# Attention and two expert layers on one core: a written order for TensorE in the first attention units, no filler matmuls, half of their copies on VectorE, narrower score weights

## The chip, the cores and the metric

The kernel runs on one core of a Trainium2 chip. The metric is the device time of one execution in microseconds. Engines are named as in the profile: PE is TensorE (PEld its weight loads), DVE VectorE, ACT ScalarE, POOL GpSimd, SP SyncE, whose queue issues nearly all transfers.

## What is computed

Inputs are q, k, v of shape (4, 8, 576, 64) and p of shape (4, 8, 32, 64), all f32.

```python
def sm_attn(qq, kk, vv):
    s = scale * np.matmul(qq, kk.transpose(0, 1, 3, 2))
    a = np.exp(s - np.max(s, axis=-1, keepdims=True))
    a = a / (np.sum(a, axis=-1, keepdims=True) + 1e-09)
    return np.matmul(a, vv)
p_packed = sm_attn(p, k, v)              # 32 packed rows per head
out = sm_attn(q, p_packed, p_packed)     # the 576 queries attend to them
x = out as (2304, 512)
h = x @ w_in                             # 512 x 2048
x = softplus(h) @ w_out                  # 2048 x 512
out = (sigmoid(x @ w_gate) * (x @ w_val)) @ w_out2    # 512 x 1536, 1536 x 512
```

## The kernel before

**Attention.** There are eight units u, one for each batch b and group g of four heads. `attn_unit(u)` is a generator of eleven stages: k is copied chunk by chunk on POOL (`by_chunk`, the tile x), transposed on PE and copied from PSUM to kT (`tr_pair`, two head pairs, one stage each, all copies on ACT as E1 is ACT); the scores of p against k (L403) go to the PSUM tile s1, of which DVE takes the maximum; ACT makes the exponential a1, DVE normalises it; q is transposed in the same way; a1 is transposed to a1T (L437); pp = a1T times v (L456) is the packed p, which ACT copies into the block diagonal tile bdT, and POOL from there into ppq (L472), whose layout holds all four batches side by side; scores of q against bdT (s2, L486), whose softmax a2 runs over DVE, ACT and POOL; last, a2 is transposed (L514) and kept as a high part A2h and a low part A2l. In the units u < WARM (3), `warm` adds six 128x128 matmuls on the identity behind pp (L381): their result goes nowhere.

**The first expert layer.** h and the product with w_out go in chunks c of 256 columns; an entry (b, c) makes two `emit_h` groups (twelve matmuls L113 to L115 each, three for each product of high and low parts) and, two groups later, the `emit_out1` of the group (L725, L726, L728, 24 matmuls), whose sums DVE adds to xa (L733). p_packed is folded into the weights: the wp of an entry are w_in times the packed rows. For c = 0 and 1 `prep_wp_one` does that for each batch (L591), for c = 3 and up `prep_wp_four(c)` does it for all four: eight matmuls of ppq with w_in (L645) in two groups, an ACT copy of each bank into a cv tile (L652), sixteen small transfers from cv to xs that put each batch's rows in place (L656), and then, in `split_wp`, POOL's high part wph (L104) and low part wpl (L101).

**Order.** Two weight buffers `raw` hold the raw words of w_in and w_out; `load_next` puts the next load on SP's queue at the end of each conversion (three DVE steps, L180, L185, L189, over a PSUM bank from some point on), since the load reuses the buffer that the conversion has emptied. Converted w_out is rounded by ACT (woh, L108) and its low part made on POOL (wol, L101). All of this is cut into generators, called jobs: `tick()` runs one step of the first job in the queue, and `between` does one tick behind every quarter of an output product. `finish("wp03")` and its like run all ticks that are still missing as soon as an entry needs its weights. Attention units get their stages from `att_tick`, which picks the next unit that is ready. The framework then orders the instructions of each engine's queue by priorities of its own, except where `tc.keep_in_program_order` pins an instruction; so an engine's order is read from the compiled program, not from the source alone.

The start is `while not att_done(1): att_tick(L0)`, with a tick each from the seventeenth on. PSUM has eight banks: four single ones (`bank1`, PSUM tile ps) that rotate, and two double ones (`bank2`).

Of the kernel before, what the change touches and what calls it, by code (L numbers as in the profile page):

```python
# [9 lines left out]
F32 = mybir.dt.float32  # L10
# [3 lines left out]
AF = mybir.ActivationFunctionType  # L14
ALU = mybir.AluOpType
# [6 lines left out]
def attn_moe_moe_kernel(  # L22
# [68 lines left out]
    def bank1():  # L91
        return ps_o[-1].tile([P, 512], F32, tag="o", name="ps1")
# [245 lines left out]
    RELD = 0  # L338
    SUMP = 0
    E1 = nc.scalar  # L340
    WARM = 3
    FOUR = 3
    SPC = 2

    def heads(tile_, start, step):
# [11 lines left out]
        )  # L357
        return x

    def tr_pair(src, j, dst, eng):  # L360
        x = by_chunk(src, j)
        for hf in range(2):
            ps = bank1()
            for c in range(3):
                nc.tensor.transpose(
                    ps[:, c * CT : (c + 1) * CT],
                    x[:, 3 * hf + c].rearrange("p h d -> p (h d)"),
                    ident[:CT, :CT],
                )
# [13 lines left out]
    def attn_unit(u):  # L383
        b, g = divmod(u, 2)
        half, odd = divmod(b, 2)
        px = bank1()
        nc.tensor.transpose(px[:, :P], praw.pop(u).rearrange("p i d -> p (i d)"), ident)
# [7 lines left out]
        tr_pair(kt, 0, kT, nc.scalar)  # L395
# [14 lines left out]
        mx = att.tile([P, 4], F32, tag="mx", bufs=2, name="mx")  # L410
        nc.vector.tensor_reduce(mx[:, 0:1], s1[:, :, :HS], op=ALU.max, axis=AX.XY)
        nc.vector.tensor_scalar(mx[:, 1:2], mx[:, 0:1], -SC, None, op0=ALU.mult)
# [9 lines left out]
        else:  # L422
            nc.vector.tensor_scalar(a1, a1, mx[:, 3:4], None, op0=ALU.mult)
        yield
        qt = kqv.pop(("q", u))
        qT = att.tile([P, 2, S], F32, tag="qT", bufs=2, name="qT")
        tr_pair(qt, 0, qT, nc.scalar)
        yield
        tr_pair(qt, 1, qT, E1)
        done_kqv("q", u)  # L430
        yield
        a1T = att.tile([CT, NC, P], F32, tag="a1T", bufs=2, name="a1T")
        for hf in range(2):
            pa = bank1()
            for c in range(3):
                o = (3 * hf + c) * CT
                nc.tensor.transpose(pa[:CT, c * P : (c + 1) * P], a1[:, o : o + CT], ident)  # L437
            nc.scalar.activation(
                a1T[:, 3 * hf : 3 * hf + 3].rearrange("p c n -> p (c n)"),
                pa[:CT, : 3 * P], AF.Copy,  # L440
            )
        yield
        vt = kqv.pop(("v", u))
        pp = bank1()
        for j in range(2):
            for c in range(NC):
                if u >= VCH:
                    nc.tensor.matmul(
                        pp[:, 64 * j : 64 * j + 64],
                        vt[:, c, 2 * j : 2 * j + 2].rearrange("p h d -> p (h d)"),  # L450
                        a1T[:, c, 64 * j : 64 * j + 64], start=c == 0, stop=c == NC - 1,
                    )
                    continue
                for e in range(2):
                    n0 = 64 * j + 32 * e
                    nc.tensor.matmul(  # L456
                        pp[64 * e : 64 * e + 64, 64 * j + 32 * e : 64 * j + 32 * e + 32],
                        vt[:, 2 * j + e, c, :],
                        a1T[:, c, n0 : n0 + 32],
                        start=c == 0,  # L460
                        stop=c == NC - 1,
                    )
        done_kqv("v", u)
        warm(u, pp[:, 3 * P :], 6)
        for e in range(2):
            r = slice(64 * e, 64 * e + 64)
            to = bdT[r].rearrange("p j n -> p (j n)")
            copy(
                BDA, heads(to, 512 * half + 256 * g + 64 * odd + 32 * e, 64 if odd else 192),
                heads(pp[r], 32 * e, 64),  # L470
            )
            nc.gpsimd.tensor_scalar(  # L472
                ppq[r, 2 * g : 2 * g + 2, b],
                heads(to, 512 * half + 256 * g + 64 * odd + 32 * e, 64 if odd else 192),
                1.0, 0.0, op0=ALU.mult, op1=ALU.add,
            )
        yield
        a2s = []
        for hf in range(2):
            s2 = bank1()  # L480
            for c in range(3):
                for j in range(2):
                    slot = odd ^ j
                    o = c * P + 64 * slot
                    t = (3 * hf + c) * CT
                    nc.tensor.matmul(  # L486
                        s2[:CT, o : o + 64],
                        qT[:, j, t : t + CT],
                        bdT[:, 4 * half + 2 * g + j, 64 * slot : 64 * slot + 64],
                        start=True,  # L490
                        stop=True,
                    )
# [18 lines left out]
        for hf in range(2):  # L511
            pt = bank1()
            for c in range(3):
                nc.tensor.transpose(  # L514
                    pt[:, c * CT : (c + 1) * CT], a2s[hf][:, c * P : (c + 1) * P],
                    ident[:CT, :CT],
                )
# [16 lines left out]
    def att_done(u):  # L534
        return att_left(u) == 0
# [2 lines left out]

    def ready(u, n):
        return n not in NEEDS or (NEEDS[n], u) in kqv  # L540

    def att_tick(last=2 * B):

# [88 lines left out]

    xs = {}

    def prep_wp_four(c):

        wt = w_in_f[c]
# [272 lines left out]
    units.extend(range(2 * B))  # L910
    n = 0
    jobs.append(("win0", prep_win(0)))
    while not att_done(1):
# [244 lines left out]
```

## Time and profile before

| | |
|---|---|
| time of 3 runs | 861.76 us median (861.45 to 863.3) |
| the profiled execution | 862.72 us, its span 860.6 us |
| PE busy | 839.2 us (98%) |
| DVE busy | 588.4 us (68%) |
| POOL busy | 479.8 us (56%) |
| ACT busy | 326.5 us (38%) |
| moved by transfers | 90.79 MB, 105 GB/s in the mean |

The span runs from the first to the last instruction. A busy share is a mean over stages that differ: in the first 42 us PE waits for loads and for the other engines, from then on it works nearly without a pause until the end.

### The profile page before, as it was taken

The numbers are of one execution on the slowest core, as the hardware profiler recorded it, in microseconds if no ns is written. First come the engines' busy times: TensorE is split into PE (matmuls) and PEld (weight loads), VectorE is DVE, ScalarE is ACT, GpSimd is POOL, SyncE is SP. The second block draws the span as 40 slices with busy tenths as digits, with TensorE's granted clock in tenths as the row PEclk, the third lists the DMA queues.
The fourth block names the chain that finished last, engine by engine and source line by source line (L and its number), as shares of the span: only waits on it lengthen the run. The fifth ranks groups of instructions, "written<-read, shape, count | busy, mean of one in ns | idle before, by whom it ended". The sixth has DMA issues, their size and how long they took to land. (4 is left out here: it accounts for less than half of the span.)

```text
span 860.6 us, 15689 instructions
## 1 busy us (share of the span) xinstructions
PE 839.2 (98%) x6112; PEld 783.0 (91%) x6112; DVE 588.4 (68%) x1004; ACT 326.5 (38%) x606; POOL 479.8 (56%) x469
## 2 busy tenths in 40 slices
PE   7899999999999999999989999999999999999997
PEld 5788989899989999999989999999989999999996
DVE  2776556946656375458788688897896656767665
ACT  4467575563333333434323422232352432322210
POOL 4564333245647364594579786886983734536400
PEclk9999999999999999999999999999999999999999
DMA  9984320203363233500155464644525412213003
GB/s 236 222 206 103 84 59 26 74 25 108 114 178 101 73 98 82 167 5 1 37 171 156 151 177 149 191 129 136 159 55 154 122 41 84 68 43 111 13 1 110
DMA packets 61864, 90.79 MB, mean 105 GB/s; under 512 B 7648, under 2 KB 40544, under 8 KB 61792
## 3 DMA queue, kind: packets, MB, share of 16 engines
q1 hardware_dynamic: 60784, 88.56, 36.9%
q10 hardware_dynamic: 1008, 1.25, 0.4%
q8 instruction: 48, 0.79, 0.4%
q14 instruction: 24, 0.20, 0.1%
HBM read 65.67 MB, written 18.87 MB: 98 GB/s over the span
## 5 line engine op out<-in xcount | busy, mean ns | idle before, releaser
L113 PE MATMUL bank<-aop,BH 128*128 128x288 f32 x672 | 199.1, 296 | 5.0 <-DVE work L1026 2.1
L115 PE MATMUL bank<-aop,BL 128*128 128x288 f32 x672 | 198.6, 296 | 0.0
L114 PE MATMUL bank<-aop,BH 128*128 128x288 f32 x672 | 197.8, 294 | 0.2 <-DVE aop L101 0.2
L733 DVE TENSOR_TENSOR xa<-xa,ps 128x288 f32<-128x288 f32 x224 | 99.5, 450 | 100.3 <-PE ps L728 100.1
L101 POOL TENSOR_TENSOR ghl<-g,ghl 128x576 fp32r<-128x576 f32 x64 | 93.5, 1463 | 132.1 <-ACT ghl L108 113.1
L725 PE MATMUL ps<-ghl,woh 128*128 128x288 f32 x512 | 146.4, 301 | 2.0 <-ACT cv L652 1.3
L726 PE MATMUL ps<-ghl,wol 128*128 128x288 f32 x512 | 143.6, 295 | 0.0
L113 PEld LDWEIGHTS bank<-aop,BH 128*128 128x128 f32 x672 | 126.2, 188 | 10.8 <-issue 2.5
L114 PEld LDWEIGHTS bank<-aop,BH 128*128 128x128 f32 x672 | 126.4, 188 | 4.2 <-DVE aop L101 0.4
L115 PEld LDWEIGHTS bank<-aop,BL 128*128 128x128 f32 x672 | 126.6, 188 | 0.0
L101 POOL TENSOR_TENSOR BL<-cv,BH 128x512 fp32r<-128x512 f32 (+1 forms) x96 | 117.2, 1235 | 3.4 <-ACT BH L108 2.4
L728 PE MATMUL ps<-ghl,woh 128*128 128x288 f32 x512 | 109.1, 294 | 0.1
L725 PEld LDWEIGHTS ps<-ghl,woh 128*128 128x128 f32 x512 | 96.2, 188 | 5.6 <-ACT cv L652 1.6
L726 PEld LDWEIGHTS ps<-ghl,wol 128*128 128x128 f32 x512 | 96.3, 188 | 0.2
L1026 DVE TENSOR_TENSOR work<-work,bank 128x576 f32<-128x576 f32 (+1 forms) x100 | 70.8, 725 | 31.5 <-PE bank L115 31.3
L1074 PE MATMUL ps<-ol,gv 128*128 128x512 f32 x216 | 84.9, 393 | 0.0
L1073 PE MATMUL ps<-oh,gv 128*128 128x512 f32 x216 | 84.3, 390 | 0.5 <-ACT gv L1039 0.4
L1075 PE MATMUL ps<-oh,gv 128*128 128x512 f32 x216 | 84.7, 393 | 0.0
L728 PEld LDWEIGHTS ps<-ghl,woh 128*128 128x128 f32 x512 | 82.2, 188 | 0.5 <-POOL ghl L101 0.5
L1081 DVE TENSOR_TENSOR xa<-xa,ps 128x512 f32<-128x512 f32 x90 | 61.5, 683 | 28.5 <-PE ps L1075 28.0
L104 POOL TENSOR_SCALAR BH<-cv 128x512 fp32r<-128x512 f32 (+1 forms) x48 | 30.0, 634 | 88.1 <-PE bank L114 87.8
L113 PE MATMUL ps<-A2h,wph 128*128 128x288 f32 x256 | 77.3, 302 | 0.4 <-ACT wph L595 0.4
(137 smaller groups left out, 1613.7 us busy)
## 6 DMA issues: line engine op xcount, KB each, us to landing
cv<-B SPq DMA_DIRECT2D x52, 256.0 KB, 2.7
B<-cv SPq DMA_DIRECT2D x48, 256.0 KB, 4.1
raw_in<-in_moe_w_in_dram SPq DMA_DIRECT2D x16, 512.0 KB, 3.7
raw_out<-in_moe_w_out_dram SPq DMA_DIRECT2D x16, 512.0 KB, 3.5
raw_g<-in_moe_w_gate_dram SPq DMA_DIRECT2D x12, 512.0 KB, 4.1
raw_v<-in_moe_w_val_dram SPq DMA_DIRECT2D x12, 512.0 KB, 4.4
raw_o<-in_moe_w_out_dram SPq DMA_DIRECT2D x12, 512.0 KB, 4.1
xs<-cv SPq DMA_DIRECT2D x80, 64.0 KB, 2.0
```

Of the source, the lines that this page charges most:

```text
L101: eng.tensor_tensor(lo, x, hi.bitcast(F32), op=ALU.subtract)
L113: nc.tensor.matmul(ps, wh, xh, start=first, stop=False)
L114: nc.tensor.matmul(ps, wh, xl, start=False, stop=False)
L115: nc.tensor.matmul(ps, wl, xh, start=False, stop=last)
L725: nc.tensor.matmul(out_, wh[:, ms], gh[:, f], start=f == 0, stop=False)
L726: nc.tensor.matmul(out_, wl[:, ms], gh[:, f], start=False, stop=False)
L728: nc.tensor.matmul(out_, wo_hl[c, f][0][:, ms], gl[:, f], start=False, stop=f == 1)
L733: nc.vector.tensor_tensor(dst, dst, out_, op=ALU.add)
L1026: nc.vector.tensor_tensor(to, x, y, op=ALU.add)
L1073: nc.tensor.matmul(bank, gh[:, ts_], oh, start=f == 0, stop=False)
L1074: nc.tensor.matmul(bank, gh[:, ts_], ol, start=False, stop=False)
L1075: nc.tensor.matmul(bank, gl[:, ts_], oh, start=False, stop=f == 1)
```

## The change

The change has five parts. (1) `FIRST` is a string that names, digit by digit, the unit whose next stage comes next, for the first 25 stages; `att_step` runs them, and while they last the PE instructions of units 0 to 2 are pinned to program order. Unit 1 (`AFIRST`) transposes its a1 ahead of its q. (2) WARM goes to 0: no fillers (FILL is empty). (3) In units 0 and 1 (`BYDVE`) DVE copies the second head pair of k and of q and the second half of a1T, which ACT did. (4) The scores of p take 64 columns of weights at a time and put each head pair into its own 64 partitions of s1, where before 128 columns, of which half belong to zeros, were accumulated over both pairs. (5) The copies into ppq leave `attn_unit` and become `prep_ppq`, eight steps ahead of `prep_wp_four` in the job of c = 3. The branch on VCH goes; its condition u >= 8 never held.

```diff
-    WARM = 3
+    WARM = 0
     FOUR = 3
+    FILL = {}
+    BYDVE = 2
+    AFIRST = (1,)
+    FIRST = "0001110000111101" + "222" + "000111"
+    pin = {u: False for u in range(2 * B)}
...
+    def pe(on, ins):
+        if on:
+            tc.keep_in_program_order(ins)
...
+        second = nc.vector if u < BYDVE else E1
...
-        tr_pair(kt, 1, kT, E1)
+        tr_pair(u, kt, 1, kT, second)
...
         for hf in range(2):
             for j in range(2):
-                nc.tensor.matmul(
-                    s1[:, hf, :HS],
-                    pT[u % 2][:, P * j : P * j + P],
+                r = slice(64 * j, 64 * j + 64)
+                pe(pin[u], nc.tensor.matmul(
+                    s1[r, hf, :HS],
+                    pT[u % 2][:, 192 * j : 192 * j + 64],
                     kT[:, j, hf * HS : (hf + 1) * HS],
-                    start=j == 0,
-                    stop=j == 1,
-                )
+                    start=True,
+                    stop=True,
+                ))
...
+                copy(
+                    hf == 0 or u >= BYDVE,
+                    a1T[:, 3 * hf : 3 * hf + 3].rearrange("p c n -> p (c n)"),
+                    pa[:CT, : 3 * P],
+                )
+        if u in AFIRST:
+            weights()
+            yield
...
-            nc.gpsimd.tensor_scalar(
-                ppq[r, 2 * g : 2 * g + 2, b],
-                heads(to, 512 * half + 256 * g + 64 * odd + 32 * e, 64 if odd else 192),
-                1.0, 0.0, op0=ALU.mult, op1=ALU.add,
-            )
...
+    def prep_ppq():
+        for b in range(B):
+            half, odd = divmod(b, 2)
+            for e in range(2):
+                r = slice(64 * e, 64 * e + 64)
+                for g in range(2):
+                    src = heads(
+                        bdT[r].rearrange("p j n -> p (j n)"),
+                        512 * half + 256 * g + 64 * odd + 32 * e, 64 if odd else 192,
+                    )
+                    pool_hi(ppq[r, 2 * g : 2 * g + 2, b], src)
+                yield
...
         if half == 0:
+            if c == FOUR:
+                yield from prep_ppq()
             yield from prep_wp_four(c)
...
+    for n, x in enumerate(FIRST):
+        for u in pin:
+            pin[u] = n < len(FIRST) and u <= 2
+        att_step(int(x))
+        if n > NW:
+            tick()
...
     while not att_done(1):
         att_tick(L0)
-        n += 1
-        if n > NW:
-            tick()
+        tick()
```

The change moves instructions at two places of the program: in the first 45 us or so, and around the weights job of c = 3, a quarter of the way through. Elsewhere every engine's order is the same as before.

The first place is DVE's order in the start, up to wpl of the first entry (cv and woh there are w_out of c = 0, mx and a the softmax of unit 2's scores, A2l the low parts of units 0 and 1). Before:

```order
L411 TENSOR_REDUCE mx<-ps_500 128x1
L101 TENSOR_TENSOR A2l_117<-ps_513,A2h_113 128x288
L412 TENSOR_SCALAR mx<-mx 128x1
L185 SCALAR_TENSOR_TENSOR cv<-raw_out,cv 128x512
L101 TENSOR_TENSOR A2l_117<-ps_519,A2h_113 128x288
L418 TENSOR_SCALAR mx<-mx 128x1
L189 SCALAR_TENSOR_TENSOR cv<-raw_out,cv 128x512
L419 RECIPROCAL mx<-mx 128x1
L101 TENSOR_TENSOR wpl<-ps_527,wph 128x512
```

And in the changed kernel, from the first conversion of w_in's second half on, and up to wpl:

```order
L180 TENSOR_SCALAR w_in<-raw_in 128x4x128
L514 TENSOR_REDUCE m_374<-ps_367 96x12
...
L438 RECIPROCAL mx<-mx 128x1
L101 TENSOR_TENSOR A2l_117<-ps_497,A2h_113 128x288
L442 TENSOR_SCALAR a_471<-a_471,mx 128x576
L189 SCALAR_TENSOR_TENSOR w_in<-raw_in,w_in 128x4x128
L101 TENSOR_TENSOR A2l_117<-ps_503,A2h_113 128x288
L180 TENSOR_SCALAR cv<-raw_out 128x512
L185 SCALAR_TENSOR_TENSOR cv<-raw_out,cv 128x512
L189 SCALAR_TENSOR_TENSOR cv<-raw_out,cv 128x512
L101 TENSOR_TENSOR wpl<-ps_511,wph 128x512
```

The conversion of w_in's second half ends late, behind most of the softmax work of units 0 and 1, and all three steps of the first w_out conversion stand ahead of wpl; from the maximum (L514) to wpl there are 36 instructions.

The second place is SP's queue around the transfers of the weights job of c = 3 (raw_in and raw_out are the loads of c = 3 and 4, raw_g the first one of the second expert layer). Before:

```order
L155 DMA raw_out<-in_moe_w_out_dram 128x1024 x2
L157 DMA raw_in<-in_moe_w_in_dram 128x4x256 x2
L656 DMA xs<-cv 32x512 x16
L155 DMA raw_out<-in_moe_w_out_dram 128x1024 x2
L157 DMA raw_g<-in_moe_w_gate_dram 128x4x256
```

And in the changed kernel:

```order
L155 DMA raw_out<-in_moe_w_out_dram 128x1024 x2
L157 DMA raw_in<-in_moe_w_in_dram 128x4x256 x2
L699 DMA xs<-cv 32x512 x8
L155 DMA raw_out<-in_moe_w_out_dram 128x1024
L699 DMA xs<-cv 32x512
L155 DMA raw_out<-in_moe_w_out_dram 128x1024
L699 DMA xs<-cv 32x512 x7
L157 DMA raw_g<-in_moe_w_gate_dram 128x4x256
```

The two raw_out loads move from behind the sixteen xs transfers to between them.

The third is POOL's order at the same place: ghl is the low part of a softplus result, on which an output product waits. Before:

```order
L101 TENSOR_TENSOR ghl<-g_2848,ghl 128x576
L104 TENSOR_SCALAR wph<-xs 128x512
L101 TENSOR_TENSOR wpl<-xs,wph 128x512
L104 TENSOR_SCALAR wph<-xs 128x512
L101 TENSOR_TENSOR wpl<-xs,wph 128x512
L104 TENSOR_SCALAR wph<-xs 128x512 x2
L101 TENSOR_TENSOR wpl<-xs,wph 128x512 x2
L101 TENSOR_TENSOR ghl<-g_2912,ghl 128x576
```

And in the changed kernel:

```order
L101 TENSOR_TENSOR ghl<-g_2792,ghl 128x576
L101 TENSOR_TENSOR wol<-cv,woh 128x512
L104 TENSOR_SCALAR wph<-xs 128x512
L101 TENSOR_TENSOR wol<-cv,woh 128x512
L101 TENSOR_TENSOR wpl<-xs,wph 128x512
L104 TENSOR_SCALAR wph<-xs 128x512 x2
L101 TENSOR_TENSOR wpl<-xs,wph 128x512 x2
L104 TENSOR_SCALAR wph<-xs 128x512
L101 TENSOR_TENSOR wpl<-xs,wph 128x512
L101 TENSOR_TENSOR ghl<-g_2898,ghl 128x576
```

The two wol of the next chunk, which stood behind three of the following ghl, now stand ahead of the first wph and of the first wpl. On PE, at the same place, the two groups of four weights matmuls (L645 before, L688 after) had 22 other matmuls between them and now have none; from the second group to the first L113 that reads the new wph there were 66 matmuls, and now there are 48.

## Rows read from the trace of the kernel before

**Rows 1.** The profile's page: busy time of PE, and the granted clock in 40 slices.

```profile
PE 839.2 (98%) x6112; PEld 783.0 (91%) x6112; DVE 588.4 (68%) x1004; ACT 326.5 (38%) x606; POOL 479.8 (56%) x469
...
PEclk9999999999999999999999999999999999999999
```

**Rows 2.** Windows: length, busy us (instructions) by engine, PE clock, DMA share, GB/s.

```profile
0.00:20.00 20.00, 15.61 (x98) 10.54 (x98) 3.30 (x9) 8.95 (x26) 9.30 (x17) 1.00 0.97 232
20.00:42.00 22.00, 18.88 (x219) 15.76 (x219) 17.68 (x45) 10.57 (x32) 11.28 (x15) 1.00 1.00 223
...
100.00:160.00 60.00, 59.53 (x587) 55.10 (x587) 38.74 (x93) 35.11 (x78) 21.52 (x26) 1.00 0.21 51
...
210.00:225.00 15.00, 15.00 (x112) 14.13 (x112) 7.47 (x18) 5.26 (x9) 6.64 (x7) 1.00 0.45 124
```

**Rows 3.** Timeline, all engines, 39 to 43 us: start, duration, what, idle before.

```profile
40.16 0.67 DVE L101 TENSOR_TENSOR wpl<-ps,wph 128x512 fp32r<-128x512 f32 x1
...
42.25 0.38 PE L115 MATMUL ps<-A2h,wpl 128*128 128x288 f32 x1
```

**Rows 4.** Timeline of PE, 50 to 52.5 us.

```profile
50.50 1.60 PE L381 MATMUL ps<-ident 128*128 128x128 f32 x12
```

**Rows 5.** Waits, 0 to 45 us: in total, times, longest.

```profile
ACT bdT L96 <- PE ps L381: 4.7, 2, 2.4
```

**Rows 6.** Groups of PE instructions by form, 42 to 165 us: busy us, mean ns.

```profile
L403 PE MATMUL ps<-kT,pT 128*128 128x288 f32 x40 | 10.7, 410 | 0.0
L591 PE MATMUL ps<-w_in,bdT 128*64 128x256 f32 x56 | 6.9, 386 | 0.2 <-ACT qT L372 0.2
```

**Rows 7.** Timeline of SP's queue, 0 to 46 us.

```profile
24.87 0.38 SPq L237 DMA_DIRECT2D xa<-in_q_dram  x1
```

**Rows 8.** Timeline of DVE, 21 to 28 us.

```profile
22.07 0.42 DVE L180 TENSOR_SCALAR w_in<-raw_in 128x512 int32<-128x512 int32 x1
```

**Rows 9.** Timeline of PE, 210 to 226 us.

```profile
210.01 1.24 PE L645 MATMUL ps<-w_in,ppq 64*128 64x256 f32 x8
...
214.30 1.13 PE L645 MATMUL ps<-w_in,ppq 64*128 64x256 f32 x8
...
224.20 0.29 PE L113 MATMUL ps<-A2h,wph 128*128 128x288 f32 x1
```

**Rows 10.** Timeline of SP's queue, 200 to 235 us.

```profile
211.84 11.01 SPq L656 DMA_DIRECT2D xs<-cv  x16
225.65 4.94 SPq L155 DMA_DIRECT2D raw_out<-in_moe_w_out_dram  x2
```

**Rows 11.** Timeline of POOL, 220 to 232 us.

```profile
222.49 0.62 POOL L104 TENSOR_SCALAR wph<-xs 128x512 fp32r<-128x512 f32 x1 [1.49 <-DMA xs<-cv]
223.19 1.29 POOL L101 TENSOR_TENSOR wpl<-xs,wph 128x512 fp32r<-128x512 f32 x1
```

**Rows 12.** Groups by form, 205 to 250 us, of DVE.

```profile
L185 DVE SCALAR_TENSOR_TENSOR ps<-raw_out,ps 128x512 int32<-128x512 int32 x4 | 2.8, 696 | 0.1
```

**Rows 13.** Groups by form, 205 to 250 us, of ACT.

```profile
L108 ACT ACTIVATE woh<-cv 128x512 fp32r<-128x512 f32 x4 | 2.5, 628 | 4.7 <-DVE cv L189 4.7
```

**Rows 14.** Groups by form, 205 to 250 us, of POOL.

```profile
L101 POOL TENSOR_TENSOR ghl<-g,ghl 128x576 fp32r<-128x576 f32 x8 | 11.4, 1431 | 13.1 <-ACT ghl L108 12.1 <-POOL wol L101 1.0
L101 POOL TENSOR_TENSOR wol<-cv,woh 128x512 fp32r<-128x512 f32 x4 | 5.2, 1294 | 1.7 <-ACT woh L108 1.7
```

**Rows 15.** The page's transfers: count, KB each, median us from issue to landing.

```profile
raw_out<-in_moe_w_out_dram SPq DMA_DIRECT2D x16, 512.0 KB, 3.5
...
xs<-cv SPq DMA_DIRECT2D x80, 64.0 KB, 2.0
```

**Rows 16.** Timeline of PE, 244 to 250 us.

```profile
248.02 0.40 PE L725 MATMUL ps<-ghl,woh 128*128 128x288 f32 x1 [1.32 <-ACT cv L652]
```

**Rows 17.** Waits, 205 to 250 us.

```profile
DVE ps L180 <- DMA raw_out<-in_moe_w_out_dram: 0.4, 2, 0.2
```

**Rows 18.** Waits of PE, 8 us to the end.

```profile
PE bank L113 <- DVE work L1026: 2.1, 2, 1.7
```

More of the change, by code (lines that the diff above doesn't have):

```diff
@@ L358, in by_chunk, with tr_pair @@
         return x
-    def tr_pair(src, j, dst, eng):
+    def pe(on, ins):
+        if on:
+            tc.keep_in_program_order(ins)
+    def tr_pair(u, src, j, dst, eng, fill=0):
+        on = pin[u]
         x = by_chunk(src, j)
@@ L363, in tr_pair @@
             ps = bank1()
+            for _ in range(0 if hf else fill):
+                pe(on, nc.tensor.matmul(
+                    ps[:, 320:], hot[:, :P], hot[:, 320:], start=True, stop=True
+                ))
             for c in range(3):
-                nc.tensor.transpose(
+                pe(on, nc.tensor.transpose(
                     ps[:, c * CT : (c + 1) * CT],
@@ L368, in tr_pair @@
                     ident[:CT, :CT],
-                )
+                ))
             o = dst[:, j, hf * HS : (hf + 1) * HS]
@@ L386, in attn_unit @@
         px = bank1()
-        nc.tensor.transpose(px[:, :P], praw.pop(u).rearrange("p i d -> p (i d)"), ident)
+        pe(pin[u], nc.tensor.transpose(
+            px[:, :P], praw.pop(u).rearrange("p i d -> p (i d)"), ident
+        ))
         for e in range(2):
@@ L392, in attn_unit @@
             )
+        second = nc.vector if u < BYDVE else E1
         kt = kqv.pop(("k", u))
         kT = att.tile([P, 2, S], F32, tag="kT", bufs=1, name="kT")
-        tr_pair(kt, 0, kT, nc.scalar)
+        tr_pair(u, kt, 0, kT, nc.scalar, FILL.get(("k", u), 0))
         yield
-        tr_pair(kt, 1, kT, E1)
+        tr_pair(u, kt, 1, kT, second)
         done_kqv("k", u)
@@ L424, in attn_unit, with weights @@
         yield
+        a1T = att.tile([CT, NC, P], F32, tag="a1T", bufs=2, name="a1T")
+        def weights():
+            for hf in range(2):
+                pa = bank1()
+                for c in range(3):
+                    o = (3 * hf + c) * CT
+                    pe(pin[u], nc.tensor.transpose(
+                        pa[:CT, c * P : (c + 1) * P], a1[:, o : o + CT], ident
+                    ))
+                copy(
[6 more added lines that the diff above has]
+            yield
         qt = kqv.pop(("q", u))
         qT = att.tile([P, 2, S], F32, tag="qT", bufs=2, name="qT")
-        tr_pair(qt, 0, qT, nc.scalar)
+        tr_pair(u, qt, 0, qT, nc.scalar, FILL.get(("q", u), 0))
         yield
-        tr_pair(qt, 1, qT, E1)
+        tr_pair(u, qt, 1, qT, second)
         done_kqv("q", u)
         yield
[L432 to L442, printed above, removed]
+        if u not in AFIRST:
+            weights()
+            yield
         vt = kqv.pop(("v", u))
@@ L446, in attn_unit @@
             for c in range(NC):
[L447 to L453, printed above, removed]
                 for e in range(2):
                     n0 = 64 * j + 32 * e
-                    nc.tensor.matmul(
+                    pe(pin[u], nc.tensor.matmul(
                         pp[64 * e : 64 * e + 64, 64 * j + 32 * e : 64 * j + 32 * e + 32],
@@ L461, in attn_unit @@
                         stop=c == NC - 1,
-                    )
+                    ))
         done_kqv("v", u)
@@ L470, in attn_unit @@
                 heads(pp[r], 32 * e, 64),
-            )
-            nc.gpsimd.tensor_scalar(
-                ppq[r, 2 * g : 2 * g + 2, b],
-                heads(to, 512 * half + 256 * g + 64 * odd + 32 * e, 64 if odd else 192),
-                1.0, 0.0, op0=ALU.mult, op1=ALU.add,
             )
@@ L485, in attn_unit @@
                     t = (3 * hf + c) * CT
-                    nc.tensor.matmul(
+                    pe(pin[u], nc.tensor.matmul(
                         s2[:CT, o : o + 64],
@@ L491, in attn_unit @@
                         stop=True,
-                    )
+                    ))
             s2v = s2[:CT, : 3 * P].rearrange("p (x n) -> p x n", n=NK)
@@ L513, in attn_unit @@
             for c in range(3):
-                nc.tensor.transpose(
+                pe(pin[u], nc.tensor.transpose(
                     pt[:, c * CT : (c + 1) * CT], a2s[hf][:, c * P : (c + 1) * P],
                     ident[:CT, :CT],
-                )
+                ))
             hi = A2h[b][:, g, hf * HS : (hf + 1) * HS]
@@ L540, in ready, with att_step @@
         return n not in NEEDS or (NEEDS[n], u) in kqv
+    def att_step(u):
+        if u in units:
+            units.remove(u)
+            live.append([attn_unit(u), 0, u])
+        x = next(y for y in live if y[2] == u)
+        next(x[0])
+        x[1] += 1
+        if x[1] == STAGES:
+            live.remove(x)
     def att_tick(last=2 * B):
@@ L633, in attn_moe_moe_kernel @@
     xs = {}
+    def prep_ppq():
[9 more added lines that the diff above has]
+                    pool_hi(ppq[r, 2 * g : 2 * g + 2, b], src)
+                yield
     def prep_wp_four(c):
@@ L912, in attn_moe_moe_kernel @@
     jobs.append(("win0", prep_win(0)))
+    for n, x in enumerate(FIRST):
[4 more added lines that the diff above has]
+            tick()
+    for u in pin:
+        pin[u] = False
     while not att_done(1):
         att_tick(L0)
-        n += 1
-        if n > NW:
-            tick()
+        tick()
     jobs.append(("wp00", prep_wp_one(0, 0)))
```

1 line of the change is left out of this document (added).

## The prediction

> **What bounds the kernel now.** I read the page first: PE is busy 839.2 us of 860.6 and its granted clock stands at 9 or more tenths in every slice [rows 1], so only PE time that goes or PE idle time that comes can move the end. Then the windows by stage [rows 2]: PE idles 4.4 us of the first 20 and 3.1 of the next 22, but 0.47 of the 60 from 100 to 160, and nothing at all from 210 to 225. So before about 42 us the start is a race of loads and VectorE work; behind it a microsecond of matmuls taken out of attention is a microsecond gained, and a stall put in is one lost. Next the timeline where the first h group gets going [rows 3]: L113 and L114 of h(0,0) have run, and its first L115 starts at 42.25, behind VectorE's wpl (40.16 + 0.67) and the transposes that stand between. From there PE hardly waits. The middle of the kernel I read last, since the order shows that the change reaches it.
>
> **What is removed.** Fillers: two groups of twelve passes stand in the start, and the third at 50.50 [rows 4], where PE is the bound; its row is 1.60 us long with the tail of its last pass, under which the next work begins, so I take 1.4. The first two cost ACT 4.7 us of waiting before its bdT copies [rows 5], which belongs to the start-up chain below and is not counted twice. The branch on VCH was never taken: nothing.
>
> **Scores.** Eight passes of L403 a unit: 40 passes are 10.7 us from 42 to 165, 2.14 a unit. The new shape (64 weight columns, alternating halves of the PSUM rows) has no row of its own; the nearest is L591, 64 weight columns into alternating halves, 56 passes in 6.9 us [rows 6], 0.123 each over 256 columns. For 288 columns that is 0.139, 1.1 us a unit. Bounds: nothing gained, if the halves don't overlap; 1.03 us a unit if they do wholly. L591 alternates its halves as the new rows will, so I take near the upper end, 0.85 (busy time counts the tail of a group's last pass, and switching remains). Five units lie where PE is the bound: 4.3 us (0 to 5.2). The three in the start hang on loads and count there.
>
> **Start-up order.** In the new order q of unit 2 is loaded ahead of raw_out, where before it stood behind it in SP's queue until 24.87 [rows 7]; the VectorE chain that ends in wpl is what the first L115 will wait for. That chain can't begin ahead of the second conversion of raw_in, which now started at 22.07 as soon as its load was there [rows 8]: the new order puts it ahead of the maximum of the first s2, and counting its 0.42 the 36 instructions from there to wpl start at about 22.5. VectorE did 45 instructions in 17.68 us busy of the 22 from 20 to 42 [rows 2], 0.39 each: 36 are 14.1 us, so wpl ends at 36.6 without any wait, and with the same share of waiting (22.0/17.68) at 40.0. Nothing tells which end is nearer; I take the middle, 38.3, and L115 moves there from 42.25: 4.0 us gained (2.2 to 5.6). VectorE's ten copies for units 0 and 1 (about 0.39 each by the same row, 3.9 us) fall into the first 22 us, of which it is busy 3.30 in the first 20 [rows 2]; if that cover were gone they would delay the chain by up to their 3.9 us, and this term would be nothing. The gains are 1.4 + 4.3 + 4.0 = 9.7 us (about 4 to 12).
>
> **The ppq copies and their eight yields.** GpSimd's sixteen small copies stay early in its order (they are only written elsewhere), so they cost nothing new. But the job that holds them eats eight ticks ahead of the weights job of chunk 3. Before, its two groups of L645 stood at 210.01 and 214.30 and the first L113 that needs the result at 224.20 [rows 9]: 14.2 us of PE work between. In the new order both groups stand together and only 48 matmuls lie between the second one and that L113. Counting from the first L688 as 0: two groups 2.4 us, then 48 at 15.00/112 = 0.134 us [rows 2], 6.4: PE comes to L113 at 8.8 and to the first L115 at 9.2.
>
> What it needs takes longer. Before, SP's sixteen xs transfers began 1.8 us after the first L645 and took 11.01 (0.69 each), and raw_out came behind all of them [rows 10]; wph started at 222.49, having waited 1.49 us for xs, which is 10.65 after the first transfer, and wpl at 223.19 [rows 11]. So by the xs train alone wph starts at 1.8 + 10.65 = 12.5 and wpl ends at 12.5 + 0.7 + 1.29 = 14.5: **5.3 us late**. That is the lower bound.
>
> The upper one is the order as it stands. SP has raw_out behind eight xs and a second raw_out behind the ninth; each waits for the VectorE conversion that empties its buffer, and the rest of xs is queued behind. GpSimd has wol, wph, wol, wpl, and each wol needs its raw_out landed, converted and rounded. Step by step (conversions about 0.70 each, ACT's rounding 0.63, wol 1.29 [rows 12 to 14], raw_out 3.5 us to landing, xs 2.0 [rows 15]): the eighth xs is issued by 1.8 + 8 x 0.69 = 7.3, the first conversion chain (three steps, with L733 of four banks between) is done at about 6; raw_out is issued at 7.3 and lands at 10.8; its three conversions and an L733 end at 13.3, ACT at 14.0, wol at 15.3, wph at 15.9. The second raw_out waits for the second chain until about 9 and lands at 12.5; its conversions come behind the first's and end at 15.8, ACT 16.4, wol 17.7, wpl **19.0 instead of 9.2, 9.8 late**. The xs themselves are there by 14, so the wols set it. Behind wpl GpSimd does three more wph, three wpl and the lo half of the first g (3 x 0.62 + 3 x 1.29 + 1.43 = 7.2), done at 26.2, while PE has 37 matmuls (5.0 us) until it wants that g, at 24.0: 2.2 more. **12.0 us lost**; by the xs train alone 5.3 + 2.2 = 7.5. I take 12.0: the row nearest to the new order is the order itself, and each wait in it has a landing or a conversion that can't come earlier. A later wait of 1.3 us, at 248.02, PE for ACT's copy of the next such job [rows 16], is likely swallowed by the delay: 10.7 net.
>
> **Sum.** 862.72 (the profiled execution's own time) - 9.7 + 10.7 = 863.7. That execution lies 0.96 above the median, so against the median: 861.76 + 1.0 = **862.8 us**, no change that can be told; 0.2%, 1.7 us, is what a measurement of this kernel can tell from none.
>
> **Rivals.** (1) *Only the xs train is late*, because the raw_out loads land and convert before PE runs dry: 4.5 us less loss, 858.3. For it: VectorE waited 0.4 us in all for raw_out from 205 to 250 [rows 17]. Against it: there it was issued behind xs, at 225.65, with time to spare. It decides when the first wol is done before wph's xs have landed. (2) *The start gives nothing* (slower): VectorE, which now takes ten more copies and whose chain holds all four s2 before wpl, is the bound of the start; wpl ends at 42.3 instead of 38.3, the loss stays, 862.8 + 4.0 = 866.8. It decides if wpl ends later than about 41. For it: VectorE was busy 17.7 of 22 us there; against it: the copies lie ahead of the stretch, and its last waits were for PE and ACT work that comes earlier now. (3) *The scores run one after the other*: 862.8 + 4.3 = 867.1. L591 speaks against it. (4) *The clock falls in the stall.* PE's longest wait now is 1.7 us [rows 18], and no slice shows a granted clock under 9 tenths [rows 1], so as far as the rows show its work goes at 2.4 GHz; the new order makes idle stretches of about 7 and 3 us. If the clock falls to 1.2 GHz in one and half of the 5.0 us of matmuls behind it run at that level, 2.5 us more are lost: 865.3. The Trainium skill, TensorE: Matmul & The Clock Gate, Part 1, says that an idle engine is throttled to half its clock and released by activity; by that rule this rival holds and the time is 865.3, while no row of before has a stretch long enough to tell. Part of it would lie under GpSimd's backlog of 2.2 us. (5) *No stall at all*: the job's transfers come in time, 862.8 - 10.7 = 852.1. Only an order that differs from the compiled one could do that.
>
> **Chances.** Forecast 0.48 (its own range 859.5 to 866.0; of it 0.06 faster, 0.26 within, 0.16 slower); rival 1 0.22 (faster 0.21); rival 2 0.12; rival 3 0.05; rival 4 0.08; rival 5 0.05. Faster by over 0.2%: 0.06 + 0.21 + 0.05 = 0.32; within, with 0.01 of rival 1: 0.27; slower 0.16 + 0.12 + 0.05 + 0.08 = 0.41. The range from 856.0 to 867.2 holds rivals 1 to 4 and leaves out rival 5 and the tails, under 0.2.
>
> **What would show it.** First L115 at 38 to 39 us; scores of eight passes in about 1.1 us; no filler rows; from the first L688 of chunk 3 some 7 us of PE waiting in all up to L113 (on wph, and on banks ahead of it) and one of nearly 3 on wpl, then one of 2 on the lo half of g, GpSimd waiting on ACT's woh ahead of them; granted clock 1.00 throughout. Wrong would be: wpl after 41, xs in time, or a PE that idles less than 6 us in that stretch.

## The result, and the profile after

The changed kernel takes **874.67 us** in the median of 4 runs (869.52 to 875.92), the kernel before 862.53 beside it (861.45 to 864.92). The ratio is 1.0126, 95% interval 1.0079 to 1.0173: slower, by some 11 us (12.1 between the medians). The profiled execution took 875.34 us with a span of 873.4, 12.8 longer than before.

The page of the changed kernel first, with the two lines that answer to [rows 1].

```profile
PE 843.1 (97%) x6076; PEld 781.3 (89%) x6076; DVE 596.8 (68%) x1014; ACT 323.9 (37%) x596; POOL 480.4 (55%) x469
...
PEclk9679999999899999999999999999999999999999
```

PE has 36 instructions fewer and is busy 3.9 us longer. That can't come from work, since work was taken out; the second line says where it comes from. Two slices, from 22 to 65 us, stand at 6 and 7 tenths of the clock, and a third, from 218 to 240, at 8, where before no slice was below 9. The windows lay this out by stage; the two in the middle answer to [rows 2].

```profile
20.00:26.00 6.00, 4.33 (x50) 4.03 (x48) 4.50 (x11) 1.24 (x5) 1.82 (x4) 1.00 1.00 224
26.00:32.00 6.00, 5.48 (x22) 3.22 (x23) 3.70 (x12) 2.23 (x6) 3.19 (x4) 0.51 1.08 272
32.00:36.00 4.00, 1.36 (x9) 0.88 (x7) 3.35 (x13) 2.24 (x6) 1.84 (x2) 0.89 0.77 161
36.00:42.00 6.00, 4.75 (x23) 3.40 (x24) 5.12 (x9) 2.15 (x6) 2.02 (x3) 0.53 0.37 113
42.00:52.00 10.00, 9.86 (x107) 8.18 (x106) 6.84 (x8) 7.64 (x18) 7.10 (x7) 0.94 0.82 215
52.00:64.00 12.00, 10.48 (x55) 8.54 (x54) 8.62 (x22) 6.01 (x14) 3.79 (x5) 0.57 0.64 175
...
100.00:160.00 60.00, 59.50 (x599) 54.20 (x597) 38.87 (x95) 37.02 (x83) 24.03 (x28) 1.00 0.21 51
...
210.00:225.00 15.00, 15.00 (x116) 14.37 (x115) 8.20 (x19) 5.78 (x10) 6.52 (x5) 1.00 0.26 81
225.00:240.00 15.00, 5.85 (x36) 4.86 (x34) 10.08 (x19) 1.26 (x2) 3.85 (x4) 0.81 0.67 196
240.00:250.00 10.00, 9.40 (x56) 9.16 (x57) 1.56 (x4) 4.02 (x6) 9.83 (x10) 0.77 0.03 9
```

Three longer windows of the same kernel are used further down.

```profile
20.00:42.00 22.00, 15.91 (x101) 11.53 (x100) 16.67 (x41) 7.87 (x23) 8.88 (x11) 0.72 0.81 196
42.00:60.00 18.00, 16.34 (x143) 13.97 (x142) 12.85 (x20) 11.78 (x28) 9.78 (x10) 0.78 0.64 175
236.00:244.00 8.00, 4.54 (x17) 4.19 (x18) 1.87 (x3) 1.21 (x2) 6.83 (x8) 0.50 0.42 132
```

From 26 to 32 us PE is busy 5.48 of 6 us with only 22 matmuls, at a granted clock of 0.51, which is the level of 1.2 GHz; the same again from 36 to 42 and from 52 to 64. Two separate losses can be read here: a slow clock in the start, and 9 us of idle PE at 225 to 240 with a slow clock behind it. The timeline of PE shows what it did ahead of each fall in the start (start, duration, what, idle time before it and its releaser; rows between those shown are left out).

```profile
24.62 0.30 PE L402 MATMUL ps<-ident,p 128*128 128x128 f32 x1 [0.60 <-PE ps L504]
26.00 0.70 PE L380 MATMUL ps<-ident,x 96*128 96x96 f32 x3 [1.08 <-POOL x L359]
...
29.11 2.62 PE L422 MATMUL ps<-kT,pT 128*64 128x288 f32 x8
...
36.36 0.74 PE L532 MATMUL ps<-ident,a 96*128 96x96 f32 x3 [2.20 <-POOL a L522]
38.00 1.98 PE L620 MATMUL ps<-w_in,bdT 128*64 128x256 f32 x8 [0.90 <-DVE w_in L189]
...
43.12 0.39 PE L115 MATMUL ps<-A2h,wpl 128*128 128x288 f32 x1
...
53.59 4.10 PE L504 MATMUL ps<-bdT,qT 128*96 128x64 f32 x24 [1.50 <-ACT bdT L96]
```

No filler stands between 20 and 42 us. PE waits 0.60 and 1.08 us ahead of 26.0, 2.20 ahead of 36.4 and 1.50 ahead of 53.6, and each time the clock is at 1.2 GHz in the matmuls that follow: the eight passes of the scores at 29.11 take 2.62 us and the 24 of s2 at 53.59 take 4.10, where before such 24 took 2.25:

```profile
53.28 2.25 PE L486 MATMUL ps<-bdT,qT 128*96 128x64 f32 x24 [0.68 <-ACT bdT L96]
```

The first L115, which was to move from 42.25 [rows 3] to 38.3, stands at 43.12.

The longest waits of PE, from 8 us to the end, answer to [rows 18] (total, times, longest):

```profile
PE ps L113 <- POOL wph L104: 6.3, 1, 6.3
PE ps L532 <- POOL a L522: 3.4, 3, 2.2
PE ps L115 <- POOL wpl L101: 2.6, 1, 2.6
PE ps L504 <- ACT bdT L96: 1.5, 1, 1.5
```

The first and the third are the stall that was forecast. This is the timeline of POOL across it, which answers to [rows 11],

```profile
234.98 1.27 POOL L101 TENSOR_TENSOR wol<-cv,woh 128x512 fp32r<-128x512 f32 x1 [14.25 <-ACT woh L108]
236.22 0.63 POOL L104 TENSOR_SCALAR wph<-xs 128x512 fp32r<-128x512 f32 x1
238.01 1.26 POOL L101 TENSOR_TENSOR wol<-cv,woh 128x512 fp32r<-128x512 f32 x1 [1.17 <-ACT woh L108]
239.24 1.26 POOL L101 TENSOR_TENSOR wpl<-xs,wph 128x512 fp32r<-128x512 f32 x1
```

and this SP's queue, which answers to [rows 10]:

```profile
222.59 5.06 SPq L699 DMA_DIRECT2D xs<-cv  x8
227.75 0.53 SPq L155 DMA_DIRECT2D raw_out<-in_moe_w_out_dram  x1
228.38 0.51 SPq L699 DMA_DIRECT2D xs<-cv  x1
229.29 0.35 SPq L155 DMA_DIRECT2D raw_out<-in_moe_w_out_dram  x1
229.69 4.31 SPq L699 DMA_DIRECT2D xs<-cv  x7
```

POOL stands for 14.25 us before a wol whose woh hangs on the raw_out issued at 227.75, and wph and wpl are queued behind the two wols. The first L688 of chunk 3 began at 220.80; wph ends at 236.85, 16.05 us later (forecast 15.9), wpl at 240.50, 19.7 us later (forecast 19.0).

The scores, in the same groups as [rows 6], from 64 to 165 us (four units):

```profile
L422 PE MATMUL ps<-kT,pT 128*64 128x288 f32 x32 | 4.8, 419 | 0.0
```

That is 1.2 us a unit, where 32 passes took 8.5 before: 0.93 saved in each, 0.85 forecast.

### The profile page after: what moved, and what is told of

Its sections match the earlier page's. It is cut to its first block, busy times and chain, and to the rows that moved or that the text cites. A ratio compares the mean times of both kernels' runs of the same rounds, so it can differ in the third digit from the quotient of the medians.

```text
span 873.4 us, 15612 instructions
## 1 busy us (share of the span) xinstructions
PE 843.1 (97%) x6076; PEld 781.3 (89%) x6076; DVE 596.8 (68%) x1014; ACT 323.9 (37%) x596; POOL 480.4 (55%) x469
## 5 line engine op out<-in xcount | busy, mean ns | idle before, releaser
L113 PE MATMUL bank<-aop,BH 128*128 128x288 f32 x672 | 199.1, 296 | 3.4 <-DVE work L1089 0.9
L115 PE MATMUL bank<-aop,BL 128*128 128x288 f32 x672 | 198.7, 296 | 0.0
L113 PEld LDWEIGHTS bank<-aop,BH 128*128 128x128 f32 x672 | 126.2, 188 | 9.2 <-POOL BL L101 1.1
L115 PEld LDWEIGHTS bank<-aop,BL 128*128 128x128 f32 x672 | 126.6, 188 | 0.0
L113 PE MATMUL ps<-A2h,wph 128*128 128x288 f32 x256 | 78.4, 306 | 6.4 <-POOL wph L104 6.3
L115 PE MATMUL ps<-A2h,wpl 128*128 128x288 f32 x256 | 77.1, 301 | 3.0 <-POOL wpl L101 2.6
```

The source lines that it names most:

```text
L113: nc.tensor.matmul(ps, wh, xh, start=first, stop=False)
L115: nc.tensor.matmul(ps, wl, xh, start=False, stop=last)
```

## The experiments

Twelve kernels were run. Where a kernel is said to be the change with an edit, the diff is against the changed kernel; otherwise against the kernel that the text names. Times are medians, beside a ratio to the kernel before on the same chip with its 95% interval. The runs were made on several chips, on which the kernel before itself has medians from 862.2 to 865.1 us, so two experiments are compared by their ratios where they ran apart.

**e1: the change without its yields.** The eight ticks go, the copies stay.

```diff
-                yield
...
-                yield from prep_ppq()
+                prep_ppq()
```

> The changed kernel with its ppq copies made in one step, without the eight yields; nothing else. Theory (the eight ticks push the weights job of c = 3 together and behind raw_out and wol): the PE stall of 6.3 + 2.6 us there and the half clock behind it vanish; about 11 us less than the changed kernel's 874.7, so 863 to 865, and still not faster than before, since the start loses 2.2 us. Rival (the stall comes from the late start or from VectorE's extra work): it stays and the time is 872 or more.

Measured: 864.64 us, 0.9989 [0.9954, 1.0023]. From 225 to 240 us PE is busy all 15.00 us: the stall is gone with the ticks. The start has falls as in the change, with a clock of 0.77 from 20 to 42 us and 0.81 from 42 to 60, and the first L115 at 42.13. So 10 to 12 us of the loss are the yields (10.0 by the medians, 11.8 by the ratios), and of the 9.7 us of gain that should have stood behind them next to nothing is left.

**e2: the change with the fillers of before** (WARM = 3, kept in the written order).

```diff
-    WARM = 0
+    WARM = 3
...
-                nc.tensor.matmul(to, ident, ident, start=True, stop=True)
+                pe(pin[u], nc.tensor.matmul(to, ident, ident, start=True, stop=True))
```

> The changed kernel with the 128x128 fillers behind pp of units 0 to 2 put back (WARM 3), everything else as changed. Theory (without fillers PE runs dry in the start, the granted clock falls to 1.2 GHz from about 26 to 43 and 54 to 63 us, and the transposes and scores on the way to wpl take twice their time): clock 1.00 in most of 20 to 64 us, the first L115 at 39 to 41, 3 to 6 us less than the changed kernel: 869 to 872. Rival (VectorE's chain sets the start, the clock only follows): first L115 still at 43, the time within 1.5 us of 874.7.

Measured: 873.67 us, 1.0088 [1.0051, 1.0125]. The first L115 is at 41.20, the clock is 0.92 from 20 to 42 us and 1.00 from 42 to 60. At 157 us the kernel is 3.7 us ahead of before, where the change is 2.2 behind: 5.9 us come back by adding 36 passes of fillers, with VectorE, ScalarE and GpSimd in another order too from 17 us on. The profiled execution, at 877.39 us one of the slower ones, loses them again at 460 to 480 us, where the clock falls to 0.83 behind a wait of 4.6 us between the two layers. The time is above the 869 to 872 that were expected, since the stall is in it.

**e3: the kernel before with the ppq job and its yields alone.**

```diff
-            nc.gpsimd.tensor_scalar(
-                ppq[r, 2 * g : 2 * g + 2, b],
...
+            if c == FOUR:
+                yield from prep_ppq()
             yield from prep_wp_four(c)
```

> The kernel before with one part of the change alone: the ppq copies as a job with eight yields. Theory: the order of SP and POOL around the weights job of c = 3 is then that of the changed kernel, the stall is there, and the time is 10 to 12 us over before, 872 to 875. Rival (the stall needs the new start): within 2 us of before.

Measured: 874.31 us, 1.0104 [1.0037, 1.0171]. The job alone makes the stall in a kernel whose start is untouched: PE's waits for wph and wpl are

```profile
PE ps L113 <- POOL wph L104: 6.2, 1, 6.2
...
PE ps L115 <- POOL wpl L101: 2.9, 1, 2.9
```

**e4: the kernel before without fillers** (WARM = 0, one line).

```diff
-    WARM = 3
+    WARM = 0
```

> The kernel before with one part of the change alone: WARM 0, no fillers. Theory: the fillers keep the clock up in the start; without them the granted clock falls somewhere in 20 to 64 us and the 1.4 us of fillers taken from the bound part are lost again or more: 862 to 867. Rival (fillers only cost): clock 1.00 throughout and 859 to 861.

Measured: 869.63 us, 1.0052 [1.0014, 1.0089]: slower. The first L115 comes 2.75 us earlier, at 39.50. The bdT copies no longer wait for fillers, and three conversion steps of VectorE that stood ahead of wpl now stand behind it; which of the two brings the gain was not tried. Then the clock is at 0.75 from 42 to 60 us, and at 157 us the kernel is 2.2 behind. The term of −1.4 us for the fillers has the wrong sign. The profiled execution took 865.0 us and is one of the fastest of the ten, so where the median loses another 4.6 us no trace shows.

**e5, e6 and e8: fillers back and no yields.** e5 is e1 and e2 together. e6 adds six matmuls ahead of each a2 group of unit 1, where PE waits for POOL. e8 is e5 with BYDVE = 0, so that ACT makes all copies.

```diff
+            for _ in range(6 if u == 1 else 0):
+                pe(pin[u], nc.tensor.matmul(
+                    pt[:, 3 * P :], ident, ident, start=True, stop=True
+                ))
```

> The changed kernel with both mends: fillers behind pp in units 0 to 2, and the ppq copies without yields. Theory (two causes that add): against the kernel with the yields alone mended (0.9989 of before) the start gains about 4 to 6 us, so 0.993 to 0.996 of before, some 4 us faster. Rival (the start is worth nothing, the clock falls by chance): within 0.2% of before.

> As the run with both mends, and twelve more fillers of 128x128 in unit 1, six ahead of each of the two groups of a2 transposes, where PE waited 1.55 and 1.67 us for GpSimd and the clock fell to 1.2 GHz behind it (36 to 40 us). Theory: the clock stays up there, the first L115 moves from 41.2 to 39 or 40, and 0.5 to 2 us are gained over the run with both mends. Rival (the fillers cost what they take): no gain, or up to 2.7 us lost.

> As the run with both mends, with all copies of units 0 and 1 on ACT as before (BYDVE 0). Theory (VectorE was idle where its copies stand): the first L115 up to 1 us later, the time within 1.5 us of the run with both mends. Rival (VectorE's ten copies delay its chain to wpl): 2 to 4 us faster than that run.

Measured: e5 862.03 us, 1.0002 [0.9977, 1.0028]; e6 859.75, 0.9959 [0.993, 0.9988]; e8 862.77, 1.0014 [0.9989, 1.0039]. e5 and e6 were expected to be faster than that: e5 gains nothing on before, and in e6 the first L115 did not move. In e5 the clock still is 0.72 from 36 to 42 us, in e6 it is 0.72 from 20 to 26 and 1.00 from 30 to 60; the first L115 stands at 41.99 in both. So a held clock behind 30 us is not by itself what brings that L115 forward. e8 differs from e5 by less than either's interval, and its first L115 is 0.83 us later: the DVE copies are not what made the start late.

**e7: the kernel before with the new scores alone.**

```diff
-                    s1[:, hf, :HS],
-                    pT[u % 2][:, P * j : P * j + P],
+                    s1[r, hf, :HS],
+                    pT[u % 2][:, 192 * j : 192 * j + 64],
```

> The kernel before with one part alone: scores of p with 64 columns of weights into halves of s1. Theory: 1.2 instead of 2.13 us a unit on PE, five units in the bound part: 4 to 5 us faster, 0.994 to 0.996 of before. Rival (the units' other engines set the pace): within 0.2%.

Measured: 864.69 us, 1.004 [1.0013, 1.0066]: slower. The first L115 comes 3.0 us later, behind a wait of 2.16 us for POOL's a ahead of an a2 transpose, and the clock is 0.84 from 42 to 52 us; by 157 us 2.2 of the 3.0 us are back. That the time saved in the start turned into waiting is one reading; but VectorE's order changed as well, from 14 us on, and the run doesn't part the two. Expected were 4 to 5 us of gain.

**e9: the fillers in the gaps.** The change without yields; no fillers behind pp of units 0 and 1, those of unit 2 back, the twelve of e6, and sixteen bf16 matmuls of 192 columns ahead of the k transposes of unit 2, where the change waited 1.08 us.

```diff
-    FILL = {}
+    FILL = {("k", 2): 16}
...
-        if u < WARM:
+        if u == 2:
```

> The changed kernel without the yields, and with fillers only where PE waited in the start: sixteen 192-column bf16 matmuls ahead of unit 2's first k transposes, six 128x128 ahead of each a2 group of unit 1, six behind pp of unit 2; none behind pp of units 0 and 1, where they hold up the packed p. Theory (the forecast chain to wpl was right at full clock, and fillers behind pp push its start back by what they win): clock 1.00 from 20 to 64 us, the first L115 at 38 to 40, 2 to 4 us faster than the run with more fillers, 855 to 858. Rival (the chain to wpl takes its 18 us at either clock): the first L115 at 42 and the time at 859 to 862.

Measured: **856.2 us, 0.9924 [0.9892, 0.9957]**, the fastest kernel here. The clock is 1.00 in all windows of the start:

```profile
26.00:32.00 6.00, 5.32 (x50) 4.42 (x50) 5.65 (x17) 3.82 (x10) 4.59 (x6) 1.00 1.06 251
...
36.00:42.00 6.00, 5.57 (x49) 4.45 (x45) 5.51 (x7) 4.41 (x12) 4.75 (x5) 1.00 0.76 243
...
52.00:64.00 12.00, 11.75 (x134) 10.40 (x132) 10.46 (x25) 7.86 (x18) 7.47 (x9) 1.00 0.90 229
```

PE is busy for about the same time as in the change, but on 50 matmuls instead of 22 from 26 to 32 us, and on 134 instead of 55 from 52 to 64. On the timeline of PE the first L115 stands at

```profile
39.02 0.38 PE L115 MATMUL ps<-A2h,wpl 128*128 128x288 f32 x1
```

3.2 us ahead of before; at 157 us the lead is 6.8 and at the end 7.8. The chain on VectorE from the first maximum to wpl is 18.4 us long in the change,

```profile
22.91 0.55 DVE L514 TENSOR_REDUCE m<-ps 96x12 f32<-96x384 f32 x1
...
40.64 0.69 DVE L101 TENSOR_TENSOR wpl<-ps,wph 128x512 fp32r<-128x512 f32 x1 [0.64 <-ACT wph L624]
```

and 15.2 us in e9:

```profile
23.35 0.55 DVE L514 TENSOR_REDUCE m<-ps 96x12 f32<-96x384 f32 x1
...
37.86 0.68 DVE L101 TENSOR_TENSOR wpl<-ps,wph 128x512 fp32r<-128x512 f32 x1
```

On PE the scores on the way take 1.39 us where they took 2.62 in the change:

```profile
29.30 1.39 PE L422 MATMUL ps<-kT,pT 128*64 128x288 f32 x8
```

The fillers changed more than the clock, though. ScalarE now has two exponentials of a2 ahead of two kT copies that stood in front of them, and VectorE has five softmax steps in another order; in the change VectorE waits 1.06 us for the second of those exponentials, at 28.82, and here it doesn't. How the 3.2 us divide between order and clock isn't shown.

**e10: one yield for each batch**, four ticks instead of eight.

```diff
-                yield
+            yield
```

> The changed kernel with four yields in place of eight (one for each batch); the two groups of L688 then stand apart, raw_out behind fourteen xs and wol behind wph. Theory (the stall comes from both groups together and from the wols ahead of wph and wpl, not from the copies' being late as such): PE waits at wph and wpl are 0 to 2 us together instead of 8.9, no half clock there. Rival (the xs train alone makes most of it): 4 us or more of waiting stay.

Measured once: 859.46 us, span 857.4. PE's waits for the same two tiles are

```profile
PE ps L115 <- POOL wpl L101: 0.6, 1, 0.6
...
PE ps L113 <- POOL wph L104: 0.4, 1, 0.4
```

and SP's queue reads

```profile
212.77 9.37 SPq L699 DMA_DIRECT2D xs<-cv  x14
222.24 0.53 SPq L155 DMA_DIRECT2D raw_out<-in_moe_w_out_dram  x1
```

With four ticks the xs train starts at 212.77, 10 us earlier than in the change, and raw_out goes behind fourteen of its transfers. So the stall comes from where the ticks put the queues and not from the copies. By how much four ticks differ from none a single run can't tell; eight against none is e11 against e9.

Up to 209 us this kernel, e1 and the change have the same order on PE, VectorE, ScalarE and GpSimd, instruction by instruction. The clock falls here between 26 and 42 us as it does there. But the third fall is missing, behind the same wait:

```profile
53.06 2.25 PE L504 MATMUL ps<-bdT,qT 128*96 128x64 f32 x24 [1.51 <-ACT bdT L96]
```

From 42 to 60 us the clock is 1.00 here against 0.78. At the first L115 this execution is 0.5 us ahead of the change, at 157 us 4.9. e1 is 2.7 ahead of the change at 157. So one and the same order stands between 2.7 us ahead of the kernel before and 2.2 behind at 157 us, with the falls of each execution.

**e11: e9 with the eight yields.**

```diff
-                prep_ppq()
+                yield from prep_ppq()
```

> The change with the fillers of e9 (six matmuls ahead of each a2 group of unit 1, sixteen short ones on k of unit 2, none behind pp of units 0 and 1) and with its eight yields. Theory: the clock of the start and the stall are two losses that add. The start then reads as in e9 (first L115 at 39.0, granted clock 1.00 to 200 us, 6.8 us ahead of before at 157 us), the stall behind it as in the change (PE waits of about 9 us for wph and wpl at 230 to 243 us), and the time is 856.2 + 10 to 11 = 866 to 867.5. Rival: an earlier start only makes PE wait longer in the stall, because the sixteen transfers and the raw_out loads come no earlier: then the waits for wph and wpl grow to 12 us or more and the time is 870 or above.

Measured: 867.28 us, 1.0051 [1.0026, 1.0075]. The first L115 is at 39.02 again, and the waits for wph and wpl are 6.3 and 2.6 us, to the digit those of the change. The two losses add: 11.1 us between e9 and e11 is the stall (11.0 by the ratios), 7.4 between e11 and the change is the start (6.5 by the ratios, and 5.6 between e9 and e1).

**e12: e9 with the old scores** (128 weight columns, two passes for each sum).

```diff
-                    s1[r, hf, :HS],
-                    pT[u % 2][:, 192 * j : 192 * j + 64],
+                    s1[:, hf, :HS],
+                    pT[u % 2][:, P * j : P * j + P],
```

> e9 with the scores of the kernel before (128 weight columns, two passes for each sum); all else as in e9. Theory of the prediction: five units behind 42 us cost 0.85 us more each where PE is the bound, so the time is 856.2 + 4.3 = 860.5, with eight passes at about 2.1 us in the rows. Rival: half of what PE saves there comes back as waiting for other engines, so 858.3. A third: the start's three units count as well, so above 861.

Measured: 867.82 us, 1.005 [1.0023, 1.0077], 11.6 above e9 and above every expectation. The timeline of PE shows that this isn't the scores alone:

```profile
21.31 1.59 PE L478 MATMUL ps<-a1T,xa 96*64 96x32 f32 x48 [1.97 <-DVE a1T L98]
22.83 7.58 PE L503 MATMUL ps<-bdT,qT 128*96 128x64 f32 x48
```

In e9 there is no such wait, and the 48 passes of s2 take 4.29 us at 21.27; here PE waits 1.97 us for a copy, and the clock is 0.50 from 26 to 32. The wait comes from VectorE's order, which changed with the scores: two conversion steps of raw_in, which wait for its load, stand ahead of the a1T copy, where in e9 they stand behind it.

```profile
19.64 0.43 DVE L180 TENSOR_SCALAR w_in<-raw_in 128x512 int32<-128x512 int32 x1 [2.49 <-DMA raw_in<-in_moe_w_in_dram]
...
20.71 0.55 DVE L98 COPY a1T<-ps 96x384 f32<-96x384 f32 x1
```

Of the twelve runs one had a mean clock of 0.999, and it took 861.4 us; the eight runs of e9 at 0.998 or more have a median of 855.8. The 5.6 us between them hold the scores and the other order together, and rest on one run.

## Why the prediction was wrong

The forecast was 862.8 us, its range up to 867.2, and the time is 874.67. Of the sum −9.7 + 10.7, the second term held and the first came out near nothing: +2.2 in the profiled execution at 157 us, −0.4 in the medians of e1, which has the same start and no stall.

- **The stall (10.7 us): right in mechanism and place, and in size with some luck.** e3 makes it alone, e1 and e10 take it away, and e9 against e11 measures it at 11.1 us. PE waits 6.3 and 2.6 us, on wph and wpl, with POOL waiting on ACT's woh ahead of them, and the tiles come within 0.7 us of the forecast times. Rival 1 (only the xs train late) is refuted: the wols set it. The clock's part of the loss, rival 4, came true inside that term: the granted clock is 0.50 from 236 to 244, and the matmuls there follow each other at 0.24 us instead of 0.13, some 2 us. The Trainium skill, TensorE: Matmul & The Clock Gate, Part 1, says that the throttled state is the default and that activity releases it; the 6.3 us of idle and the 0.50 behind it agree. In exchange PE no longer waited for the lo half of g, for which 2.2 us had been counted. That the sum fits is luck in this part: a wait that didn't come and a slow clock that was priced only as a rival cancel.
- **The scores (−4.3 us): the size per unit right** (0.93 against 0.85). Rival 3 is refuted by it. At the end it is worth less than forecast: in the traces of e2, e5, e6, e9 and e11, with a clock of 1.00 from 42 to 160 us and the fillers of unit 2 in place, the lead over before grows by 2.6 to 3.6 us between the first L115 and 157 us. No run has the scores alone in an unchanged order.
- **The start (−4.0 us) and the fillers (−1.4 us): the step that failed.** The prediction took the fillers as work that goes, "so I take 1.4", and as 4.7 us of waiting ahead of bdT that goes too; it counted 36 VectorE steps from the first s2 to wpl at the rates of the kernel before. Both leave out what the clock then does. The chain was to start at 22.5 and did so nearly, its first maximum at 22.91; it was to take 15.8 us and took 18.4, while in e9, with the same steps in a slightly other order and at a clock of 1.00, it took 15.2. wpl ends at 41.33, so the sign that was named for rival 2 came (wpl after 41), but not its reason: without the DVE copies the start is no faster (e8), and VectorE is busy 16.67 of the 22 us from 20 to 42, less than before. What grew are PE's steps at 1.2 GHz: the scores take 2.62 us against 1.39 in e9, the first six a2 transposes 1.22 against 0.71, the eight weights passes 1.98 against 1.08. A smaller slip is in the same term: it put L115 at the end of wpl, though before 1.4 us of other matmuls stood between them; in the change it is 1.8, in e9 0.5.
- **Where the clock rival was looked for.** The prediction asked whether the clock falls in the stall, where an idle stretch of 7 us was forecast. It didn't ask it of the start, where its own rows showed PE idle for 4.4 of 20 and 3.1 of 22 us [rows 2] with the fillers in place, and where the change took away 36 passes of fillers and shortened the rest. "Granted clock 1.00 throughout" was given as what would show it right, and it is 0.72 from 20 to 42 us and 0.78 from 42 to 60. The four kernels without fillers (the change, e1, e4, e10) all have a fall ahead of 60 us, e9 and e11 with fillers in the gaps have none, as before and e3 have none. Fillers don't ensure that: e2, e5, e6, e7, e8 and e12 have them and a fall there too.

At a held clock the start and the scores give 6.8 us by 157 us (e9) against 9.7 forecast: 3.2 up to the first L115 where 4.0 were forecast, 3.6 behind it where 4.3 were, and nothing for the third group of fillers, which e9 keeps (1.4). The 1.0 that comes up to the end is gained behind 400 us. With fillers in the gaps of the start the change takes 867.3 us (e11); the 6 to 7 us above that are what the start without them costs. How much of it is the clock and how much the order that came with the fillers is open up to the first L115. Behind it the change and e10 part by 4.4 us in the same order, and there the granted clock, 0.78 against 1.00 from 42 to 60 us, is what the rows show to differ.

## What to carry to other kernels

A matmul whose result goes nowhere has two sides: its own time, and the clock of what follows. Before fillers go, look in the trace for what PE would do in their place, and try them in the gaps rather than behind work that others wait for (ratios of 1.0002 in e5 and 0.9924 in e9 here, though number and order differ too). An edit on one engine can reorder the others: the experiments on fillers and scores changed VectorE's order as well, so compare the orders before calling a difference the effect of the edit. In a queue of generators a yield is a place in every other engine's order: compare the compiled order for one yield more and one less before pricing the work between them.

## What the runs showed that had not been expected

- Falls stand behind waits of 1.5 to 2.2 us too, and the length of the wait alone doesn't decide. The wait of 1.97 us in e12 was followed by a granted clock of 0.57 from 22 to 34 us, that of 1.50 in the change by 0.50 from 54 to 62. Yet in e10 the same wait of 1.51 us was followed by 1.00, and in the kernel before the wait of 1.7 us of [rows 18] was followed by no fall either: the clock is 1.00 from 440 to 500 us.
- That place, between the two layers, spreads the runs. From 460 to 480 us the clock falls to 0.83, 0.88 and 0.83 in the profiled executions of e2, e5 and e12, and is 1.00 in those of before, e6 and e8. Of 22 runs of the kernel before, 17 had a mean clock of 0.998 or more and took 861.6 to 863.8 us with one exception, the other five 864.6 to 868.2. What decides it in a run was not found.
- Falls come in a row. In the change three of them follow each other between 26 and 64 us: matmuls at 1.2 GHz reach the other engines late, and PE waits for them again. That one fall causes the next was not tried by itself.
